# Moving one pair's casts and stores in tile one, and starting tile zero's small products with the other PSUM bank

## The chip, the cores and the metric

The kernel runs on one core of a Trainium2 chip. The metric is device time in microseconds: the median of the runs of one program, 899.4 us for the kernel before (899.08 to 900.18 in three runs).

## The reference, cut to what matters

Attention within chunks of 64 tokens, then RMS norm and a gated feed-forward layer. Everything is f32.

```python
# q, k, v: (8, 8, 576, 64); chunk = 64, 9 chunks per sequence
scores = scale * np.matmul(q_c, k_c.transpose(0, 1, 2, 4, 3))
scores = scores - np.max(scores, axis=-1, keepdims=True)
attn = np.exp(scores)
attn = attn / (np.sum(attn, axis=-1, keepdims=True) + 1e-09)
out = np.matmul(attn, v_c)
...
# x: (4608, 512), w_gate and w_val: (512, 1536), w_out: (1536, 512)
rms = np.sqrt(np.mean(x * x, axis=-1, keepdims=True) + 1e-06)
xn = x / rms * rms_g
g = xn @ w_gate
silu = g * (1.0 / (1.0 + np.exp(-g)))
val = xn @ w_val
return (silu * val @ w_out).astype(np.float32)
```

## The kernel before, in words

The 4608 tokens are nine tiles of 512. A tile holds the tokens of two *units* of 256; a unit u is loaded (`load_unit`, `load_values`), and its attention runs as scores, softmax, transposed weights, values, norm. Each matrix of the layer is split into a high and a low part (names ending in `h` and `l`), and every product is three matmuls of 128x512: high by high, high by low, low by high.

Tile zero is computed while the weights are still being converted (`conv_step`), and the order of its work is found by a scheduler that goes by priorities; in twelve *f* steps it makes `ps_g` and `ps_v` (L601), multiplies them and adds into four banks `acc` (L689). Units 2 and 3 are attended in it: their scores (L288), transposes (L349) and values (L472) are the *small products* between the large ones. Each of these slots writes two PSUM banks, one per half `j` of the partitions (`two_banks`: `banks[0]` for j = 0, `banks[1]` for j = 1), and `in_turn` holds the slot's instructions of units 2 and 3 in the order of the program. DVE reads the values out of the two banks in `norm_unit` (L521), two instructions for j = 0 and then two for j = 1.

Tiles one and two (`gated_pair`, L666) run in an order that is written out by hand, for PE, SP, DVE, ACT and POOL. They have 48 *steps* between them: a step is the twelve matmuls of one `ps_g` (even steps) or one `ps_v` (odd steps), and behind them whatever the tables put at that step. `ps_g` has two banks (pool `ps_h`), so the `ps_g` of step k+4 needs the `silu` (L679) of step k to be done; `ps_v` has four. The tables:

- `UNIT_AT`, one row for each of units 4 to 9: the steps of load, scores and softmax, load of the values, sums and first turn, two DMAs there and back through DRAM, values and norm (`turned_values`, `turned_norm`: L412, L426, L485), scaling, second turn, two more DMAs. The pool `ps_a` has two banks, which hold the scores of one unit or the values of another. So the next unit's scores wait until the norm of the unit before has let go of both: DVE scales the values out of them (L426), and ACT then squares into them (L485).
- `SUM_AT`, one row for each of six *pairs* i of output weights: sums on DVE (L719, L727), the split (ACT cast L731, DVE L732), the store `wol` (L736).
- `SIDE_AT`, one row for each of six pairs i of input weights: `whole` and `sums` on POOL (L755), then twice a split (ACT casts `side` L782, DVE `ab` L783) and its store `wsd` (L788, L789). `whole` takes a buffer from the pool `wts`, which hands out the buffers of earlier tiles as they come free.

`do` puts a closure at a step; those of one step run in the order in which they were entered (a step with .5 goes ahead of the following step's others). Units are entered first. All DMAs of these tables are issued by SP, in that order, and every engine runs its own queue in order. The lines that matter below, beside the functions that follow:

```python
        ri = mean_squares(halves, [st["o"].rearrange("p (a q) -> p a q", q=Q) for st in subs])
...
    ps_a = ctx.enter_context(tc.tile_pool(name="ps_a", bufs=2, space=bass.MemoryType.PSUM))
```

Of the kernel before, what the change touches and what calls it, by code (L numbers as in the profile page):

```python
# [48 lines left out]
)  # L49
SIDE_AT = (  # L50
    (1, 2, 3, 4, 3, 4),
    (6, 7, 7.5, 9, 9, 10),
    (10, 12, 14, 15, 16, 17),
    (15, 17, 19, 20, 21, 22),
    (25, 27, 29, 30, 31, 32),
    (30, 32, 34, 35, 36, 37),
# [20 lines left out]
NPR = NF // 2  # L77
# [32 lines left out]
def tile_chunk_attn_swiglu(  # L110
# [9 lines left out]
    nc = tc.nc  # L120
# [36 lines left out]
    def bank(pool, name):  # L157
        return pool.tile([P, 512], F32, tag=pool_tag[id(pool)], name=name)
# [3 lines left out]
    ident = const.tile([P, P], F32, name="ident")  # L162
# [81 lines left out]
    state = {}  # L244

    def load_unit(u):
        t = io.tile([P, 2, NPAIR, UT], F32, tag="qk", bufs=1, name="qk")
        nc.sync.dma_start(t, qk[u])
        for s in range(2):
            state[2 * u + s] = {"q": t[:, 0], "k": t[:, 1]}  # L250

    def load_values(u):
        vt = io.tile([P, NPAIR, UT // CH, D], F32, tag="io", name="vt")
        nc.sync.dma_start(vt, v[u])
        for s in range(2):
            state[2 * u + s]["v"] = vt
# [10 lines left out]
    def two_banks(pool, name):  # L267
        return [bank(pool, f"{name}{j}").rearrange("p (s c) -> p s c", s=2) for j in range(2)]
# [3 lines left out]
    def in_turn(i, ins):  # L272

        if 4 <= i < 8:
            if turn_last[0] is not None:
                info = mybir.DependencyInfo(mybir.DependencyClass.NoSync, mybir.DependencyReason.DATA)
                tc.add_manual_dep(ins.ins, turn_last[0].ins.name, info, reason="row groups take turns")
            turn_last[0] = ins

    def scores(i, banks):  # L280
        st, s = state[i], i % 2
        st["s"] = [b[:, s].rearrange("p (a k) -> p a k", k=CH) for b in banks]
        for pr in range(NPAIR):
            for j in range(2):
                for c in range(2):
                    tok = s * P + c * CH
                    rows = slice(j * D, (j + 1) * D)
                    ins = nc.tensor.matmul(  # L288
                        st["s"][j][c * CH : (c + 1) * CH, pr],
                        st["q"][rows, pr, tok : tok + CH],  # L290
                        st["k"][rows, pr, tok : tok + CH],
                        start=True,
                        stop=True,
                    )
                    in_turn(i, ins)
# [45 lines left out]
    def att_transpose(i, pool=None):  # L341
        st = state[i]
        e = st["e"].rearrange("p a j k -> p a (j k)")
        if i % 2 == 0:
            state["eT", i // 2] = att.tile([P, 2, NPAIR, P], F32, tag="eT", bufs=1, name="eT")
        eT = st["eT"] = state["eT", i // 2][:, i % 2]
        pt = bank(pool or ps_a, "ps_t").rearrange("p (a k) -> p a k", k=P)
        for pr in range(NPAIR):
            nc.tensor.transpose(pt[:, pr], e[:, pr], ident)  # L349
        nc.scalar.copy(eT, pt)  # L350


# [111 lines left out]
    def att_values(i, banks):  # L464
        st, s = state[i], i % 2
        eT, vt = st["eT"], st["v"]
        st["o"] = [b[:, s].rearrange("p (a d) -> p a d", d=D) for b in banks]
        for pr in range(NPAIR):
            for j in range(2):
                for c in range(2):  # L470
                    rows = slice(j * CH, (j + 1) * CH)
                    ins = nc.tensor.matmul(  # L472
                        st["o"][j][c * CH : (c + 1) * CH, pr, :],
                        eT[rows, pr, c * CH : (c + 1) * CH],
                        vt[rows, pr, 2 * s + c, :],
                        start=True,
                        stop=True,
                    )
                    in_turn(i, ins)
# [85 lines left out]
    def behind(ins):  # L565

        info = mybir.DependencyInfo(mybir.DependencyClass.Sync, mybir.DependencyReason.DATA)
        tc.add_manual_dep(ins.ins, split_last[0].ins.name, info, reason="tokens are split first")
        return ins
# [180 lines left out]
    def sides(i, st):  # L750

        at, ws = {}, []

        def total(out, one, two, op):
            return nc.gpsimd.tensor_tensor(out, one, two, op=op)  # L755

        def whole():
            ws = big([P, 2, 2, DM], F32, "ab")
            for f in range(2):
                hi, lo = (conv_parts[2 * i + f][:, n].bitcast(F32) for n in range(2))  # L760
                for half in range(2):
                    cols = slice(half * KH, (half + 1) * KH)
                    for m in range(2):
                        behind(total(ws[:, f, m, cols], hi[:, m, cols], lo[:, m, cols], ALU.add))
                    at[f + 1, half + 1] = ws[:, f, :, cols]

        def sums():
            for m in range(2):
                a = {n: w[:, m] for n, w in at.items()}
                total(a[2, 2], a[2, 1], a[2, 2], ALU.add)  # L770
                total(a[2, 1], a[1, 1], a[2, 1], ALU.subtract)
                total(a[1, 1], a[2, 2], a[1, 1], ALU.subtract)
                total(a[1, 2], a[1, 2], a[1, 1], ALU.subtract)

        forms = ((P7, (2, 1)), (P5, (2, 2))), ((P6, (1, 1)), (P3, (1, 2)))
        parts = {}

        def split(k):
            for p, n in forms[k]:
                w = at[n]  # L780
                part = parts[p] = st().tile([P, 2, KH], F32R, tag="side", bufs=4, name="side")
                nc.scalar.copy(part, w)  # L782
                nc.vector.tensor_tensor(w.bitcast(F32R), w, part.bitcast(F32), op=ALU.subtract)  # L783

        def save(k):
            for p, n in forms[k]:
                dst = wsd[:, 7 * i + p].rearrange("p (a m c) -> p a m c", a=2, m=2)
                nc.sync.dma_start(dst[:, 0], parts[p].bitcast(F32))  # L788
                nc.sync.dma_start(dst[:, 1], at[n])  # L789

        return [whole, sums, lambda: split(0), lambda: save(0), lambda: split(1), lambda: save(1)]

    def big(shape, dtype, name):
        return wts.tile(shape, dtype, tag="wts", name=name)
# [385 lines left out]
    for f in range(NF):  # L1180
        g = gated(f, CONVS[f % 2], conv_step)
        for u, at in enumerate(TILE1_AT, 2):
            if f == at[0]:
                load_unit(u)
                load_values(u)
                sc = two_banks(ps_a, "ps_s")
                for i in (2 * u, 2 * u + 1):
                    scores(i, sc)
                softmax_rows(u, sc)
            elif f == at[1]:  # L1190
                for i in (2 * u, 2 * u + 1):
                    att_transpose(i)
            elif f == at[2]:
                o = two_banks(ps_a, "ps_o")
                for i in (2 * u, 2 * u + 1):
                    att_values(i, o)
                scale[u] = norm_unit(u, o)
            elif f == at[3]:
                scale[u]()
        if f % 2:  # L1200
            save_out(f // 2)
        if f >= 6:
            save_up(f - 6)
        if f >= NF - 1 - EARLY_SUMS and f < NF - 1:
            for todo in out_sides(f - NF + 1 + EARLY_SUMS, lambda: wp.tile([P, 2 * DM], F32, name="w")):
                todo()
        if f == NF - 1:
            load_unit(4)
            x_transpose((0, 1))
        if prev is not None:  # L1210
            down(acc, f - 1, *prev)
        prev = g
# [19 lines left out]
    def do(k, f):  # L1232
        if k >= 4 * NF:
            down_at.setdefault(2 * (k - 4 * NF), []).append(f)
        elif k % 1:
            ahead.setdefault(int(k) + 1, []).append(f)
        else:
            at.setdefault(max(k, 0), []).append(f)
# [17 lines left out]
    for i in range(NPR):  # L1256
        for k, f in () if i < EARLY_SUMS else zip(SUM_AT[i], out_sides(i, lambda: st[0].tile([P, 2 * DM], F32, tag="ab", bufs=1, name="w"))):
            do(k, f)
        for k, f in zip(SIDE_AT[i], sides(i, lambda: st[0])):
            do(k, f)  # L1260
        do(P5_AT[i], lambda i=i: less_first(i))
# [31 lines left out]
    for b in range(-1, NB):  # L1293
# [7 lines left out]
        if not last_pair:  # L1301
            u = 2 * t + 4
# [98 lines left out]
```

## Time and profile before

| what | value |
|---|---|
| median of three runs | 899.4 us |
| the profiled execution's own time | 897.51 us |
| its span, first to last instruction | 895.7 us |
| PE busy | 874.6 us (98%) |
| DVE busy | 661.9 us (74%) |
| ACT busy | 438.7 us (49%) |
| POOL busy | 161.9 us (18%) |

The profiled execution lies 1.9 us below the median of the runs. A matmul's end is modelled, so PE's busy share says little; what is read in the prediction is the distance from one start to the next. In tiles one and two 128x512 matmuls start 0.23 us apart when nothing holds them up. In a row of the timeline the first number is the start in us from the beginning of the span, the second the length, and what stands in brackets is the time for which the engine sat idle ahead of it and what ended that. Rows of equal instructions are merged (x64).

### The profile page before, as it was taken

Reading aid. Unit: us, or ns where it says so; the run is one execution under the profiler, and the core shown is the slowest. Engines: PE = TensorE matmul, PEld = TensorE weight load, DVE = VectorE, ACT = ScalarE, POOL = GpSimd, SP = SyncE. Lnnn points to the kernel's source line nnn. Section 1 sums busy time; section 2 is a strip of 40 time slices with the busy share of each in tenths; the row PEclk is TensorE's granted clock in tenths of the full one; section 3 lists DMA queues with packets and bytes.
Section 4 is the critical chain, followed back from the end, with each engine's and each line's share of the span. In section 5 each row is a group of like instructions: output and inputs, shape, how many; then the busy total and the mean of one; then the engine's idle time right before and its main releaser. Section 6 shows DMA issues by size and latency. Waiting matters only on the chain.

```text
span 895.7 us, 17004 instructions
## 1 busy us (share of the span) xinstructions
PE 874.6 (98%) x6816; PEld 717.0 (80%) x6816; DVE 661.9 (74%) x971; ACT 438.7 (49%) x723; POOL 161.9 (18%) x185
## 2 busy tenths in 40 slices
PE   5899999999999999999999999999999999999998
PEld 4777878877888888888888888788888888888886
DVE  6899997877685887866757988666669973435885
ACT  5999955445452763333445644333546532112442
POOL 0000005666660000112220001222200012111000
PEclk9999999999999999999999999999999999999999
DMA  9698967789898867488986874898888687445523
GB/s 359 257 338 312 352 217 259 253 290 295 250 287 288 275 224 272 171 316 282 350 271 225 291 275 164 306 327 308 287 233 304 248 306 271 154 149 191 208 70 119
DMA packets 94495, 231.81 MB, mean 259 GB/s; under 512 B 7120, under 2 KB 63440, under 8 KB 79056
## 3 DMA queue, kind: packets, MB, share of 16 engines
q1 hardware_dynamic: 93360, 230.19, 73.8%
q8 instruction: 54, 0.88, 0.4%
q10 hardware_dynamic: 1056, 0.52, 0.2%
q14 instruction: 25, 0.20, 0.1%
HBM read 171.97 MB, written 58.72 MB: 258 GB/s over the span
## 4 chain that ended last, share of the span: by engine, by line
PE 78%; ACT 7%; DVE 6%; POOL 4%; DMA 3%; issue 2%; SPq 0%; ACTq 0%; DVEq 0%; POOLq 0%
PE ps_c L854 11%; PE ps_a L854 11%; PE ps_b L854 10%; PE ps_a L1035 7%; PE ps_b L1035 7%; PE ps_c L1035 7%; PE ps_d L854 6%; PE ps_g L666 4%; PE ps_v L666 4%; PE ps_d L1035 4%; POOL ab L755 3%; PE ps_o L412 2%; PE ps_s L288 2%; PE ps_g L601 1%; PE acc L689 1%
## 5 line engine op out<-in xcount | busy, mean ns | idle before, releaser
L954 ACT CAST gh<-g 128x512 fp32r<-128x512 f32 x140 | 81.7, 619 | 75.6 <-PE ps_b L1035 21.3
L955 DVE TENSOR_TENSOR gl<-g,gh 128x512 fp32r<-128x512 f32 x140 | 95.2, 686 | 30.8 <-ACT gh L954 29.7
L854 PE MATMUL ps_c<-xp,wr 128*128 128x512 f32 x432 | 104.6, 391 | 0.0
L854 PE MATMUL ps_b<-xp,wr 128*128 128x512 f32 x432 | 104.1, 390 | 0.0
L854 PE MATMUL ps_a<-xp,wr 128*128 128x512 f32 x432 | 103.5, 390 | 0.0
L854 PEld LDWEIGHTS ps_a<-xp,wr 128*128 128x128 f32 x432 | 80.9, 188 | 16.9
L854 PEld LDWEIGHTS ps_b<-xp,wr 128*128 128x128 f32 x432 | 80.8, 188 | 16.9
L854 PEld LDWEIGHTS ps_c<-xp,wr 128*128 128x128 f32 x432 | 80.6, 188 | 17.1
L919 POOL TENSOR_TENSOR g<-c,c 128x512 f32<-128x512 f32 x18 | 23.2, 1290 | 363.0 <-ACT c L895 175.2
L666 PE MATMUL ps_g<-xh,parts 128*128 128x512 f32 x192 | 65.1, 393 | 1.7 <-ACT sg L679 1.7
L666 PE MATMUL ps_v<-xh,parts 128*128 128x512 f32 x192 | 65.5, 394 | 0.0
L1035 PE MATMUL ps_a<-gh,wo 128*128 128x512 f32 x176 | 55.8, 389 | 0.0
L854 PE MATMUL ps_d<-xp,wr 128*128 128x512 f32 x216 | 52.3, 391 | 0.4 <-DMA wr<-wsd 0.4
L895 ACT ACTIVATE c<-c 128x512 f32<-128x512 f32 x18 | 11.4, 633 | 81.2 <-DVE c L915 81.1
L1035 PE MATMUL ps_c<-gh,wo 128*128 128x512 f32 x160 | 50.8, 391 | 0.0
L1035 PE MATMUL ps_b<-gh,wo 128*128 128x512 f32 x160 | 50.6, 389 | 0.0
L755 POOL TENSOR_TENSOR ab<-parts 128x256 f32<-128x256 f32 x48 | 41.9, 909 | 33.9 <-DVE xl L559 26.2
L854 PEld LDWEIGHTS ps_d<-xp,wr 128*128 128x128 f32 x216 | 40.3, 188 | 9.3 <-issue 0.8
L997 DVE TENSOR_TENSOR g<-g 128x512 f32<-128x512 f32 x68 | 46.4, 683 | 0.0
L904 DVE TENSOR_TENSOR u<-ps_b,p 128x512 f32<-128x512 f32 x36 | 24.6, 689 | 29.1 <-PE ps_b L854 24.1
L666 PEld LDWEIGHTS ps_g<-xh,parts 128*128 128x128 f32 x192 | 36.0, 188 | 9.9 <-ACT sg L679 2.1
L666 PEld LDWEIGHTS ps_v<-xh,parts 128*128 128x128 f32 x192 | 36.0, 188 | 7.9
(184 smaller groups left out, 1846.3 us busy)
## 6 DMA issues: line engine op xcount, KB each, us to landing
wr<-wsd SPq DMA_DIRECT2D x63, 1024.0 KB, 8.3
qk<-qk_dram SPq DMA_DIRECT2D x17, 1024.0 KB, 6.8
wo<-wol SPq DMA_DIRECT2D x16, 1024.0 KB, 9.0
raw<-w_up_dram SPq DMA_DIRECT2D x12, 1024.0 KB, 12.0
wo<-wod SPq DMA_DIRECT2D x12, 1024.0 KB, 8.9
vt<-v_dram SPq DMA_DIRECT2D x18, 512.0 KB, 7.8
wsd<-parts SPq DMA_DIRECT2D x18, 512.0 KB, 8.9
wo<-wol SPq DMA_DIRECT2D x16, 512.0 KB, 8.0
```

The lines of the kernel that those rows point to most:

```text
L288: ins = nc.tensor.matmul(st["s"][j][c * CH : (c + 1) * CH, pr], st["q"][rows, pr, tok : tok + CH], st["k"][rows, pr, tok : tok + CH], star ...
L412: nc.tensor.matmul(st["o"][(2 * c + t) * Q : (2 * c + t + 1) * Q, h * D : (h + 1) * D], eT[rows, c, t, h], vt[rows, c, h], start=True, sto ...
L666: nc.tensor.matmul(ps[k], a, b[dt], start=(dt == 0 and i == 0), stop=(dt == NDT - 1 and i == 2), skip_group_check=True,)
L755: return nc.gpsimd.tensor_tensor(out, one, two, op=op)
L854: nc.tensor.matmul(ps, w[:, a, m, cols], xp[:, b, kt], start=start and kt == 0 and i == 0, stop=stop and kt == 1 and i == 2, skip_group_ch ...
L895: nc.scalar.activation(t, t if src is None else src, AF.Silu)
L904: nc.vector.tensor_tensor(kp["u2"], b["b"], kp["p1"], op=add)
L919: nc.gpsimd.tensor_tensor(g[1][1], kp["c22"], kept[0]["c22"], op=mult)
L954: nc.scalar.copy(gh, src)
L955: nc.vector.tensor_tensor(gl, src, gh.bitcast(F32), op=ALU.subtract)
L997: nc.vector.tensor_tensor(out, one, two, op=ALU.subtract)
L1035: nc.tensor.matmul(ps[m][INTO[p]], w[:, m, a], parts[c], start=p in FROM and i == 0 and j == 0, stop=p in LAST and i == NPR - 1 and j == 2 ...
```

## The change

In `UNIT_AT` the fourth row (unit 7) loads its queries and keys at step 11 and not 12; its values and norm go from step 32 to 33, its scaling and second turn from 34 to 35, the store behind them from 35 to 36. In `SIDE_AT` the third row (pair 2) has its two splits at 16 and 17, not 14 and 16, and their stores at 17 and 18, not 15 and 17. All rows of `SUM_AT` are now entered ahead of all rows of `SIDE_AT`. In tile zero the small products of units 2 and 3 (i = 4 to 7) begin with j = 1, the transposes too are held in turn, and the second half of the unit is transposed first.

```diff
-    (12, 15, 27, 17, 19, 27, 32, 34, 34, 35, 38),
+    (11, 15, 27, 17, 19, 27, 33, 35, 35, 36, 38),
...
-    (10, 12, 14, 15, 16, 17),
+    (10, 12, 16, 17, 17, 18),
...
+    def halves_of(i):
+        return (1, 0) if 4 <= i < 8 else (0, 1)
...
         for pr in range(NPAIR):
-            for j in range(2):
+            for j in halves_of(i):
...
-        if i % 2 == 0:
+        if ("eT", i // 2) not in state:
...
-            nc.tensor.transpose(pt[:, pr], e[:, pr], ident)
+            in_turn(i, nc.tensor.transpose(pt[:, pr], e[:, pr], ident))
...
-                for i in (2 * u, 2 * u + 1):
+                for i in (2 * u + 1, 2 * u):
                     att_transpose(i)
...
     for i in range(NPR):
         for k, f in () if i < EARLY_SUMS else zip(SUM_AT[i], out_sides(i, ...)):
             do(k, f)
+    for i in range(NPR):
         for k, f in zip(SIDE_AT[i], sides(i, lambda: st[0])):
             do(k, f)
```

What this does to the queues is shown at three places. Lines of the changed kernel are three higher than those before. The first place is DVE in tile one, steps 7 to 9: `parts_775` is output pair 2, `ab_1762` input pair 1, `xu_1893` the norm of unit 4. Before, and then now:

```order
L727 TENSOR_TENSOR w_1796<-w_1796 128x256 x4
L783 TENSOR_TENSOR ab_1762<-ab_1762,side_1819 128x2x256
L783 TENSOR_TENSOR ab_1762<-ab_1762,side_1822 128x2x256
L732 TENSOR_TENSOR parts_775<-w_1796,parts_775 128x1024
L426 TENSOR_TENSOR xu_1893<-ps_o_1827,rs_u_1613 128x16x32
```

```order
L730 TENSOR_TENSOR w_1788<-w_1788 128x256 x4
L735 TENSOR_TENSOR parts_775<-w_1788,parts_775 128x1024
L786 TENSOR_TENSOR ab_1762<-ab_1762,side_1821 128x2x256
L786 TENSOR_TENSOR ab_1762<-ab_1762,side_1824 128x2x256
L429 TENSOR_TENSOR xu_1893<-ps_o_1827,rs_u_1613 128x16x32
```

The split of output pair 2 now stands ahead of the first split of input pair 1, and its store `wol` likewise on SP. The second place is ACT in steps 14 to 18: `e_128` is the softmax of unit 7, the `side` casts are those of input pair 2, `sg` is the `silu` of step 16. Before, and then now:

```order
L438 ACTIVATE xu_2101<-xu_2101,ri_t_2107 128x16x32 x2
L782 CAST side_2171<-ab_1995 128x512
L782 CAST side_2174<-ab_1995 128x512
L368 ACT_TABLE_LOAD
L368 ACTIVATE e_128<-e_128 128x1024
L679 ACT_TABLE_LOAD
L679 ACTIVATE sg_2250<-ps_g_2248 128x512
```

```order
L441 ACTIVATE xu_2103<-xu_2103,ri_t_2109 128x16x32 x2
L371 ACT_TABLE_LOAD
L371 ACTIVATE e_128<-e_128 128x1024
L682 ACT_TABLE_LOAD
L682 ACTIVATE sg_2240<-ps_g_2238 128x512
L785 CAST side_2261<-ab_1995 128x512
```

The four casts now stand behind that `silu`; on DVE `ab_1995` has likewise gone behind the softmax of unit 7. The third place is DVE in steps 31 to 34: `ab_2535` is input pair 4, `w` and `parts_1313` output pair 5, `xu` the norm of unit 7, `mx_u` the softmax of unit 9. Before, and then now:

```order
L783 TENSOR_TENSOR ab_2535<-ab_2535,side_2736 128x2x256
L426 TENSOR_TENSOR xu_2822<-ps_o_2756,rs_u_2294 128x16x32
L426 TENSOR_TENSOR xu_2822<-ps_o_2757,rs_u_2294 128x16x32
L719 TENSOR_TENSOR w_2837<-parts_1313 128x1024
L727 TENSOR_TENSOR w_2837<-w_2837 128x256 x4
L681 TENSOR_TENSOR g_2739<-ps_v_2741,sg_2742 128x512
```

```order
L786 TENSOR_TENSOR ab_2535<-ab_2535,side_2736 128x2x256
L722 TENSOR_TENSOR w_2758<-parts_1313 128x1024
L730 TENSOR_TENSOR w_2758<-w_2758 128x256 x4
L684 TENSOR_TENSOR g_2739<-ps_v_2741,sg_2742 128x512
L429 TENSOR_TENSOR xu_2855<-ps_o_2789,rs_u_2284 128x16x32
L429 TENSOR_TENSOR xu_2855<-ps_o_2790,rs_u_2284 128x16x32
```

The norm of unit 7 now stands behind the sums of output pair 5, where it stood ahead of them. On PE the values of unit 7 have gone from behind the `ps_g` of step 32 to behind the `ps_v` of step 33, and the scores of unit 9 still follow the `ps_g` of step 34. On SP the load of unit 7 has the same neighbours as before, since no DMA stood between its old place and its new one.

More of the change, by code (lines that the diff above doesn't have):

```diff
@@ L468, in att_values @@
         for pr in range(NPAIR):
-            for j in range(2):
+            for j in halves_of(i):
                 for c in range(2):
```

## The prediction

> **What bounds the kernel now.** I read the page first, then the waits of PE, then PE's timeline at the places that the change touches, and there the timelines of the engines that PE waits for.
>
> ```profile
> span 895.7 us, 17004 instructions
> PE 874.6 (98%) x6816; PEld 717.0 (80%) x6816; DVE 661.9 (74%) x971; ACT 438.7 (49%) x723; POOL 161.9 (18%) x185
> ```
>
> PE's waits, of all the span behind its first 40 us, the largest sum (us in total, times, longest):
>
> ```profile
> PE ps_g L666 <- ACT sg L679: 1.7, 1, 1.7
> ```
>
> PE is the bound, and with six smaller rows those waits add to 4.7 us. No matmul is added or removed. So the change is worth what it takes from these few waits, less the new ones that it makes. PE in tiles one and two, at the touched places:
>
> ```profile
> 178.40 1.39 PE L288 MATMUL ps_s<-qk 64*64 64x64 f32 x64
> 179.72 0.50 PE L666 MATMUL ps_v<-xh,parts 128*128 128x512 f32 x1
> ...
> 196.08 1.16 PE L288 MATMUL ps_s<-qk 64*64 64x64 f32 x64 [0.81 <-DMA qk<-qk_dram]
> ...
> 210.09 0.50 PE L666 MATMUL ps_g<-xh,parts 128*128 128x512 f32 x1 [1.72 <-ACT sg L679]
> 210.42 0.39 PE L666 MATMUL ps_g<-xl,parts 128*128 128x512 f32 x1
> ...
> 256.15 1.16 PE L288 MATMUL ps_s<-qk 64*64 64x64 f32 x64
> 257.24 0.50 PE L666 MATMUL ps_v<-xh,parts 128*128 128x512 f32 x1
> ```
>
> These are, in order, the scores of unit 6 (step 10), those of unit 7 (step 15, 0.81 us late for their load), the `ps_g` of step 20 (1.72 late) and the scores of unit 9 (step 34). Scores take 1.16 where nothing disturbs them; those of unit 6 took 1.39, so they were held in their middle for 0.23.
>
> **Term A, scores of unit 6.** That hold is for their second PSUM bank.
>
> ```profile
> 172.43 1.80 DVE L727 TENSOR_TENSOR w<-w 128x256 f32<-128x256 f32 x4
> 174.15 1.28 DVE L783 TENSOR_TENSOR ab<-ab,side 128x512 fp32r<-128x512 f32 x2
> 175.35 1.23 DVE L732 TENSOR_TENSOR parts<-w,parts 128x1024 fp32r<-128x1024 f32 x1
> 176.49 1.28 DVE L426 TENSOR_TENSOR xu<-ps_o,rs_u 128x512 f32<-128x512 f32 x2
> ```
>
> ```profile
> 174.26 1.05 ACT L731 CAST parts<-w 128x1024 fp32r<-128x1024 f32 x1 [1.21 <-DVE w L727]
> ```
>
> ```profile
> 177.87 0.60 ACT L485 ACTIVATE ps_o<-xu 128x512 f32<-128x512 f32 x1
> ```
>
> The norm of unit 4 starts at 176.49, its second square ends at 178.47, and the `ps_v` behind the scores starts at 179.72, 1.25 later. Now DVE does L732 first. That waits for the cast that ends at 175.31, so it starts at 175.35 as before; the two `ab`, which filled the gap, come behind it and push the norm by their distance, 175.35 - 174.15 = 1.20. Squares and bank move by as much: PE loses 1.2 us. Bounds: 0.9 if part of the `ab` still fits in the gap, 1.3 for their whole length.
>
> **Term B, the load of unit 7.** Moved from step 12 to 11 it passes no DMA on SP, so it starts no sooner.
>
> ```profile
> 180.43 2.04 SPq L736 DMA_DIRECT2D wol<-parts  x2
> ```
>
> ```profile
> 187.74 0.61 SPq L248 DMA_DIRECT2D qk<-qk_dram  x1
> ```
>
> SP spent 7.3 us on these two `wol` and five more issues between the rows; now `wol` goes ahead of all eight `wsd` stores, not between them, with the same bytes ahead of the load. So I leave the load where it was. PE comes 1.2 later by term A, more than the 0.81, and the wait is gone: a gain of 0.8. Bounds: 0 if the load lands as much later, 0.9 with the slower start behind a wait.
>
> **Term C, step 20.** The chain behind its 1.72 us:
>
> ```profile
> 187.40 7.02 POOL L755 TENSOR_TENSOR ab<-parts 128x256 f32<-128x256 f32 x8 [7.71 <-DMA wol<-parts]
> ```
>
> ```profile
> 197.99 1.25 DVE L444 STREAM_TRANSPOSE xu<-xu 128x1024 f32<-128x1024 f32 x1 [0.48 <-ACT xu L438]
> ```
>
> ```profile
> 201.29 1.14 ACT L782 CAST side<-ab 128x512 fp32r<-128x512 f32 x2 [3.33 <-POOL ab L755]
> ```
>
> ```profile
> 207.06 1.06 ACT L368 ACTIVATE e<-e 128x1024 f32<-128x1024 f32 x1 [3.33 <-DVE e L362]
> ```
>
> ```profile
> 209.44 0.60 ACT L679 ACTIVATE sg<-ps_g 128x512 f32<-128x512 f32 x1
> ```
>
> POOL waits until `wol` of pair 2 has landed, the casts wait for POOL, DVE's `ab` waits for the casts ahead of the softmax of unit 7, and the `silu` of step 16 waits for that softmax. Now casts and `ab` stand behind. DVE is through with its turn at 199.24; then come one L681 and the softmax's four instructions, some 0.6 to 0.7 each (3.4 in all), so the exponential starts near 202.7, not 207.06, and the `silu`, 2.38 behind it as before, near 205.1. PE asks for it at 210.09 - 1.72 = 208.4: it is 3 us early. The gain is 1.7, with the slower restart (0.33 instead of 0.23 to the next start, and some hundredths of semaphore time) 1.9. Bounds: 1.7 and 2.0. That `wol` and so POOL come sooner only widens this.
>
> **Term D, the turn to tile two.**
>
> ```profile
> 221.12 0.39 PE L666 MATMUL ps_g<-xh,parts 128*128 128x512 f32 x1
> 221.59 0.50 PE L666 MATMUL ps_g<-xl,parts 128*128 128x512 f32 x1
> ```
>
> The second matmul starts 0.47 behind the first, not 0.23: ACT's split of the new tile comes behind casts of pair 3, which had waited for POOL and for stores. With POOL sooner I take a gain of 0.2; pair 2's stores are a step later, so the bounds are 0 and 0.4.
>
> **Term E, scores of unit 9.** The values of unit 7 end one step ahead of the scores that need their two banks, not two, and the norm has gone behind the sums of pair 5.
>
> ```profile
> 252.77 1.28 DVE L426 TENSOR_TENSOR xu<-ps_o,rs_u 128x512 f32<-128x512 f32 x2
> 253.97 1.21 DVE L719 TENSOR_TENSOR w<-parts 128x1024 f32<-128x1024 f32 x1
> 255.21 2.22 DVE L727 TENSOR_TENSOR w<-w 128x256 f32<-128x256 f32 x4
> 257.35 0.68 DVE L681 TENSOR_TENSOR g<-ps_v,sg 128x512 f32<-128x512 f32 x1
> ```
>
> ```profile
> 192.10 3.06 DVE L727 TENSOR_TENSOR w<-w 128x256 f32<-128x256 f32 x4
> ```
>
> ```profile
> 256.18 7.49 POOL L755 TENSOR_TENSOR ab<-ab 128x256 f32<-128x256 f32 x8
> ```
>
> Until 252.77 nothing differs relative to PE. Then L719 and L727 take 253.97 to 257.35, which is 3.4, and L681 0.6, so the norm starts at 256.75. By term A's distances its squares end 1.98 later and the next `ps_v` starts 1.25 after that, at 259.98, where it was 257.24: PE loses 2.7. But POOL's sums no longer wait for this norm, so they run beside DVE's from the start; beside POOL (187.40 and on) four L727 took 3.06, against 1.80 with POOL idle and 2.22 here. With 3.06 the loss is 3.6. I take 3.4, nearer to that since POOL is busy throughout; bounds 2.7 and 4.0. Nothing gives it back: the list of waits has none of PE between here and 292 us to take it from.
>
> **Term F, tile zero.** The values of unit 2 were cut in two pieces and are now one.
>
> ```profile
> 76.42 0.33 PE L288 MATMUL ps_s<-qk 64*64 64x64 f32 x4
> ```
>
> ```profile
> 75.90 1.08 DVE L521 TENSOR_TENSOR x<-ps_o,rs_u 128x256 f32<-128x256 f32 x3
> ```
>
> ```profile
> 81.94 0.60 ACT L643 ACTIVATE sg<-ps_g 128x512 f32<-128x512 f32 x1 [0.18 <-PE ps_g L601]
> ```
>
> ```profile
> 96.21 1.23 DVE L229 TENSOR_TENSOR parts<-w,parts 128x1024 fp32r<-128x1024 f32 x1 [0.18 <-ACT parts L223]
> ```
>
> ```profile
> 126.06 0.74 PE L601 MATMUL ps_g<-xh,parts 128*128 128x512 f32 x2 [0.24 <-DVE parts L229]
> ```
>
> That saves a change of shape. But the scores of unit 3 are still cut after their first few, and the first piece now asks for the bank of j = 1. Of the three reads in the DVE row the first is the last of j = 0, the others are j = 1: with 1.08 for three, bank 0 is free at 76.3 and bank 1 at 76.98, 0.67 later. DVE sets that time, so PE stands until 0.67 later than before, and whatever the values won is lost in that wait. The delay goes on through ACT, which waits for PE at 81.94, to DVE, which waits for ACT at 96.21, to PE, which waits for DVE at 126.06. I take a loss of 0.6; bounds 0 (ACT or DVE has slack on the way) and 0.7. That the transposes of unit 3 are cut once more I cost at nothing: the two banks they write are their own. Tile one's DMAs start from PE and shift along.
>
> **Sum.** A +1.2, B -0.8, C -1.9, D -0.2, E +3.4, F +0.6: +2.3 us. Against the profiled execution's 897.5 that is 899.8; against the median of 899.4, from which this execution lies 1.9 below, 901.7.
>
> **Rivals.**
>
> 1. *No wait at the scores of unit 9.* If DVE reaches the norm of unit 7 by 254.0 (256.75 - 2.74), E is nothing: 898.3, not slower; between 254.0 and 256.75 it is in part. For it speaks that DVE's casts of pair 4 just ahead wait for POOL, which the change makes earlier in tile one; against it that POOL's work on that pair begins behind the norm of unit 6, which waits for PE, so that an earlier POOL does not move it:
>
> ```profile
> 230.72 0.34 POOL L487 TENSOR_SCALAR ms<-ms 128x2 f32<-128x2 f32 x1 [14.48 <-ACT ps_o L485]
> ```
>
> 2. *The load of unit 7 lands later.* With `wol` first, it costs from 0.4 of delay on (1.2 - 0.81); at 1.4 of delay B is +0.2 and not -0.8: 902.7. For it speaks SP's slow pace, against it the equal bytes.
>
> 3. *POOL shuts DVE out.* If each of DVE's five sums of pair 5 waits for a whole POOL operation of 7.49 / 8 = 0.94, the norm comes 1.21 + 1.80 + 4.7 + 0.6 behind 252.77, E is 7.1, and the time 905.4. Against it: the four at 192.10 lost 1.26, not 3.7. [...]
>
> 4. *PE slows behind its wait.* E would be the longest wait since the start. If the twelve matmuls behind it start twice as far apart, 12 x 0.23 = 2.7 is added: 904.4. Against it: behind 1.72 us the next start came after 0.33. [...]
>
> **How the numbers follow.** Forecast 0.63, rival 1 0.21 (in whole or part), rival 2 0.08, rival 3 0.03, rival 4 0.05. A change under 0.2% (1.8 us) can hardly be told from none. The forecast's bounds, A to F all low (0.9 - 0.9 - 2.0 - 0.4 + 2.7 + 0) and all high (1.3 + 0 - 1.7 + 0 + 4.0 + 0.7), are +0.3 and +4.3: 899.7 to 903.7. Rival 1 reaches down to 896.9 with F at 0. I take 898.4 to 903.4, which leaves out half of rival 1, the forecast's last corner, and rivals 3 and 4. Slower by over 0.2% (above 901.2): 0.6 of the forecast, and rivals 2 to 4, 0.54; less for rival 1's upper part taken as likelier, 0.50. Faster by as much (below 897.6): over half of rival 1's whole case, 0.12. No difference: 0.38.
>
> **What would show it.** The `ps_g` of step 20 without idle time; scores of unit 6 near 2.4 us long or later by 1.2, those of unit 7 without a wait for their load; scores of unit 9 held for 2.7 us or more, with the norm of unit 7 on DVE behind the sums of pair 5; `wol` of pair 2 ahead of its `wsd` neighbours and POOL's next sums 2 to 4 us sooner; in tile zero one piece of values of unit 2, and PE idle for some 0.9 ahead of the scores of unit 3. I am wrong above all if DVE reaches the norm of unit 7 early, or if PE's later start in tile one moves the loads less than PE.

## The result and the profile after

The changed kernel takes 905.33 us (median of 6 runs), the kernel before 899.24: a ratio of 1.0070, 95% interval 1.0052 to 1.0089, and outside the forecast range of 898.4 to 903.4. Measured again beside the experiments it took 903.36 against 898.57: 1.0044 (1.0030 to 1.0059). So the change costs 4 to 6 us. The side was forecast, the size (+2.3) was not. The second comparison lies at the upper edge of that range; why the two sets of six runs differ by 2 us stays open.

Two executions of the changed kernel were recorded, with spans of 905.3 and 901.5 us against 895.7 before. The page of the first, and PE's two largest waits in it behind the first 40 us (us in total, times, longest):

```profile
span 905.3 us, 17007 instructions
PE 878.2 (97%) x6816; PEld 720.4 (80%) x6816; DVE 665.2 (73%) x971; ACT 438.8 (48%) x723; POOL 160.7 (18%) x185
...
PE ps_s L291 <- ACT ps_o L488: 4.9, 3, 3.8
PE ps_s L291 <- DMA qk<-qk_dram: 2.2, 1, 2.2
```

The wait at the `ps_g` of step 20 is gone from this list. Of the two waits ahead of scores (L291 is L288 before) the first is new, and the second was 0.81 before. PE's timeline at the places that the prediction named, in the first recorded execution:

```profile
179.13 0.33 PE L291 MATMUL ps_s<-qk 64*64 64x64 f32 x4 [0.70 <-ACT ps_o L488]
179.79 1.15 PE L291 MATMUL ps_s<-qk 64*64 64x64 f32 x60 [0.33 <-ACT ps_o L488]
180.87 0.50 PE L669 MATMUL ps_v<-xh,parts 128*128 128x512 f32 x1
...
196.06 0.39 PE L669 MATMUL ps_v<-xh,parts 128*128 128x512 f32 x1
198.68 1.42 PE L291 MATMUL ps_s<-qk 64*64 64x64 f32 x64 [2.24 <-DMA qk<-qk_dram]
200.03 0.79 PE L669 MATMUL ps_g<-xh,parts 128*128 128x512 f32 x1
200.62 0.63 PE L669 MATMUL ps_g<-xl,parts 128*128 128x512 f32 x1
...
257.51 0.39 PE L669 MATMUL ps_g<-xh,parts 128*128 128x512 f32 x1
261.73 2.59 PE L291 MATMUL ps_s<-qk 64*64 64x64 f32 x64 [3.82 <-ACT ps_o L488]
264.24 0.79 PE L669 MATMUL ps_v<-xh,parts 128*128 128x512 f32 x1
264.83 0.63 PE L669 MATMUL ps_v<-xl,parts 128*128 128x512 f32 x1
```

Unit 6's scores come late by term A (`ps_v` at 180.87, not 179.72). Unit 7's wait for their load 2.24 us, and the large matmuls behind them start 0.59 and then 0.43 us apart, where 0.23 is usual. Unit 9's wait 3.82 us, take 2.59 instead of 1.16, and the matmuls behind them are slow in the same way. The windows of half a microsecond at the edges of these slow stretches (the third number from the end of a row is PE's granted clock):

```profile
199.00:199.50 0.50, 0.50 (x48) 0.50 (x42) 0.50 (x1) 0.50 (x2) 0.42 (x2) 0.91 0.15 57
202.50:203.00 0.50, 0.50 (x3) 0.39 (x2) 0.47 (x2) 0.00 (x0) 0.50 (x2) 0.68 0.93 352
260.50:261.00 0.50, 0.00 (x0) 0.00 (x0) 0.50 (x2) 0.05 (x1) 0.50 (x1) 0.85 1.06 219
267.50:268.00 0.50, 0.50 (x4) 0.41 (x2) 0.00 (x0) 0.50 (x1) 0.00 (x0) 0.82 0.03 6
```

Between these edges the granted clock is 0.50. A mean of 0.91 over half a microsecond with 1.0 ahead and 0.5 behind puts the fall at 199.41; by the same working it rises at 202.82, falls at 260.85 and rises at 267.68. In the recorded execution of before its mean from 40 to 895 us is 1.00. That is one execution: over whole executions, the first 40 us included, the mean clock of before lies between 0.994 and 1.000 in the 29 that ran beside the first experiments, and that of the changed kernel between 0.994 and 0.998 in all twelve.

DVE and POOL ahead of unit 9's scores:

```profile
254.49 1.75 DVE L722 TENSOR_TENSOR w<-parts 128x1024 f32<-128x1024 f32 x1
256.27 3.45 DVE L730 TENSOR_TENSOR w<-w 128x256 f32<-128x256 f32 x4
259.64 0.68 DVE L684 TENSOR_TENSOR g<-ps_v,sg 128x512 f32<-128x512 f32 x1
260.24 1.27 DVE L429 TENSOR_TENSOR xu<-ps_o,rs_u 128x512 f32<-128x512 f32 x2
```

```profile
255.12 5.99 POOL L758 TENSOR_TENSOR ab<-ab 128x256 f32<-128x256 f32 x6
```

The norm of unit 7 (L429) stands behind the sums as forecast, but these take 5.15 us up to the product behind them (254.49 to 259.64), not the 3.38 of before: the four L730 start 0.87 us apart on average, and so do POOL's instructions beside them (256.91 to 258.65).

**Where the time went.** The table compares the start of the same matmul (by its number on PE) with that before, in the recorded executions. Each column is what PE lost in that stretch: up to the end of tile zero, from there to behind unit 6's scores (A), behind unit 7's (B), the `ps_g` of step 20 (C), the turn to tile two (D), then all the rest but the stretch of unit 9's scores (E). The sum is the difference of the spans. Kernels that appear further down stand in it too.

| recorded execution | tile 0 | A | B | C | D | E | rest | sum |
|---|---|---|---|---|---|---|---|---|
| forecast | +0.6 | +1.2 | -0.8 | -1.9 | -0.2 | +3.4 | 0 | +2.3 |
| after, first | -0.0 | +1.2 | +3.0 | -1.9 | -0.4 | +7.0 | +0.7 | +9.6 |
| after, second | 0.0 | +1.2 | -0.1 | -1.9 | +0.2 | +6.6 | -0.2 | +5.8 |
| after_values32 | +0.2 | +1.2 | -0.9 | -1.9 | +0.9 | 0.0 | +0.5 | 0.0 |
| after_pool33 | +0.6 | +1.2 | -0.9 | -1.9 | +0.9 | +4.5 | +0.9 | +5.3 |
| after_sums33 | 0.0 | +1.2 | -0.9 | -1.9 | +0.8 | +0.2 | -0.1 | -0.8 |
| after_fill | +0.8 | +1.2 | +1.2 | -1.9 | -0.4 | +4.6 | -0.4 | +5.0 |
| after_values32_fill | 0.0 | +1.2 | +0.3 | -1.9 | -0.3 | +3.6 | -0.7 | +2.3 |
| before_loops | +0.3 | +1.2 | -0.4 | -1.3 | +0.7 | 0.0 | +0.2 | +0.8 |
| before_zero | +0.4 | 0.0 | +0.8 | -1.1 | -0.3 | 0.0 | +2.2 | +2.0 |
| before_side | +0.6 | 0.0 | +1.1 | -1.9 | -0.4 | 0.0 | +2.3 | +1.6 |
| before_side_load | -0.1 | 0.0 | -0.9 | -1.9 | +1.0 | 0.0 | -0.3 | -2.1 |
| before_side_load2 | 0.0 | 0.0 | -0.9 | -1.9 | -0.4 | 0.0 | +1.7 | -1.6 |

Of the tile zero column, up to 0.8 is scatter ahead of 40 us; the rest column is mostly waits of later tiles for a load of weights (`wr`) or ahead of a unit's values, which come and go from one execution to the next. The recorded execution of before (897.51 us) lies 1.7 below the median of the six runs of before, so the sums come out higher than the measured differences. E alone exceeds the measured slowdown.

### The profile page after: what moved, and what is told of

Its sections match the earlier page's. It is cut to its first block, busy times and chain, and to the rows that moved or that the text cites. A ratio compares the mean times of both kernels' runs of the same rounds, so it can differ in the third digit from the quotient of the medians.

```text
span 905.3 us, 17007 instructions
## 1 busy us (share of the span) xinstructions
PE 878.2 (97%) x6816; PEld 720.4 (80%) x6816; DVE 665.2 (73%) x971; ACT 438.8 (48%) x723; POOL 160.7 (18%) x185
## 4 chain that ended last, share of the span: by engine, by line
PE 66%; DMA 2%; ACT 1%; DVE 1%; SPq 0%; issue 0%; POOL 0%; ACTq 0%
PE ps_c L857 10%; PE ps_b L857 10%; PE ps_a L857 10%; PE ps_b L1038 7%; PE ps_a L1038 7%; PE ps_c L1038 7%; PE ps_d L857 5%; PE ps_d L1038 4%; PE ps_v L669 2%; PE ps_g L669 2%; PE ps_o L415 1%; DMA wr<-wsd 1%; PE ps_s L291 1%; DMA away_x<-xu 1%; DMA x<-away_x 0%
## 5 line engine op out<-in xcount | busy, mean ns | idle before, releaser
L758 POOL TENSOR_TENSOR ab<-parts 128x256 f32<-128x256 f32 x48 | 40.0, 871 | 31.0 <-DVE xl L562 26.2
```

## The experiments

**The changed kernel once more.**

> The changed kernel once more, for a second profiled execution. Theory 1 (the load of unit 7 lands too late by an amount that varies, and the clock falls behind each long wait of PE): the time is again about 905.3 us with a spread of 3 us or more, the scores of unit 9 wait 3.8 us again because DVE and POOL set that wait, but the wait for the load of unit 7 differs from 2.24 us by up to 1.5 us, and where it is under about 1.7 us (the wait that left the granted clock at 1.0 before the change) the clock stays at 1.0 behind it. Theory 2 (the order of the stores fixes the landing): the load is late by 2.2 us again, within 0.2.

903.36 us, ratio 1.0044 (1.0030 to 1.0059). Unit 9's scores waited 3.76 us, within 0.1 of the first time, and the clock fell again (0.50 from 257.74 to 264.56). The wait for the load of unit 7 was 0.69 and not 2.24, and the clock stayed at 1.0 there: the execution's mean of 0.996 is what the 6.82 us at 0.50 make of it by themselves. PE at unit 9:

```profile
255.19 0.39 PE L669 MATMUL ps_g<-xh,parts 128*128 128x512 f32 x1
259.33 2.58 PE L291 MATMUL ps_s<-qk 64*64 64x64 f32 x64 [3.76 <-ACT ps_o L488]
```

In the trace this is theory 1. The times are not what it expected: they are 2 us lower, and spread over 1.4 us, not 3. From issue to landing this load took, by the trace, 10.1 and 9.3 us in these two executions, 8.2 before, and 7.7 to 10.4 in the other kernels where it has the same neighbours on SP.

**Term E undone, in two ways.** The values of unit 7 back at their step:

```diff
-    (11, 15, 27, 17, 19, 27, 33, 35, 35, 36, 38),
+    (11, 15, 27, 17, 19, 27, 32, 34, 34, 35, 38),
```

> The changed kernel with the values and the norm of unit 7 (and its scaling, second turn and store) put back to their steps before, 32, 34, 34 and 35. Theory 1 (the move of this norm costs 2.7 for DVE's sums ahead of it, 1.8 for their slowing beside POOL, 2.4 for the fallen clock, 6.9 us in all): no wait at the scores of unit 9, the granted clock stays at 1.0 there, and the time is 905.3 - 6.9 = 898.4 us. Theory 2 (the forecast's 3.4 for this term was right and the rest went elsewhere): 901.9 us.

897.07 us, ratio 0.9979 (0.9968 to 0.9991): 6.3 us less than the changed kernel, and a little faster than before. No wait at unit 9's scores, clock 1.0:

```profile
255.67 1.16 PE L291 MATMUL ps_s<-qk 64*64 64x64 f32 x64
256.76 0.50 PE L669 MATMUL ps_v<-xh,parts 128*128 128x512 f32 x1
```

Then the values at step 33 as changed, but DVE's sums of output pair 5 behind them:

```diff
-SUM_AT = (), (), (7, 7.5, 9), (12, 13, 15), (26, 27, 29), (32, 33, 35)
+SUM_AT = (), (), (7, 7.5, 9), (12, 13, 15), (26, 27, 29), (33, 34, 35)
```

> The changed kernel with DVE's sums of output pair 5 at step 33 and its split at 34, so that the norm of unit 7 goes ahead of the five sums, with the values still at step 33. Theory 1 (the order of norm and sums on DVE is the whole of the lost 6.9 us): no wait over 0.5 us at the scores of unit 9, the granted clock at 1.0, and about 6.7 us less than the changed kernel, 896.7 us. Theory 2 (the values that end one step later cost by themselves, or the sums then hold the softmax of unit 9 and PE waits behind it): a wait of 1 us or more there or within five steps, 898 to 901 us.

897.57 us, ratio 0.9993 (0.9980 to 1.0005). DVE in it:

```profile
252.50 1.27 DVE L429 TENSOR_TENSOR xu<-ps_o,rs_u 128x512 f32<-128x512 f32 x2
253.70 1.46 DVE L722 TENSOR_TENSOR w<-parts 128x1024 f32<-128x1024 f32 x1
255.19 3.46 DVE L730 TENSOR_TENSOR w<-w 128x256 f32<-128x256 f32 x4
```

The sums are nearly as slow beside POOL as in the changed kernel (4.9 us up to the instruction behind them, 253.70 to 258.58, where it was 5.15), but behind the norm they cost PE 0.2 us at most. So neither the later values nor the slow sums cost by themselves: it is the norm's place behind the sums.

**POOL's part of E.**

```diff
-    (30, 32, 34, 35, 36, 37),
+    (30, 33, 34, 35, 36, 37),
```

> The changed kernel with one number moved: POOL's sums of input pair 5 at step 33 and not 32, so that they stand behind the norm of unit 7 as before the change, and DVE's sums of output pair 5 run with POOL idle in part. Theory 1 (POOL slows those five DVE instructions): L722 and the four L730 take 3.4 us again and not 5.15, the wait at the scores of unit 9 falls from 3.8 to about 2.0 us, and the time is 1.8 us less by the wait alone (903.5), up to 4.2 us less if the granted clock stays at 1.0 too (901.1). Theory 2 (they are slow from DMA or from their own place): their lengths and the time stay, 905.3 us.

901.66 us, ratio 1.0034 (1.0014 to 1.0055), 1.7 below the changed kernel; the intervals overlap, so the trace has to carry the verdict. DVE and then PE in it:

```profile
252.58 1.74 DVE L722 TENSOR_TENSOR w<-parts 128x1024 f32<-128x1024 f32 x1
254.36 1.80 DVE L730 TENSOR_TENSOR w<-w 128x256 f32<-128x256 f32 x4
256.08 0.68 DVE L684 TENSOR_TENSOR g<-ps_v,sg 128x512 f32<-128x512 f32 x1
```

```profile
258.17 0.33 PE L291 MATMUL ps_s<-qk 64*64 64x64 f32 x4 [2.12 <-ACT ps_o L488]
258.79 1.71 PE L291 MATMUL ps_s<-qk 64*64 64x64 f32 x60 [0.28 <-ACT ps_o L488]
260.43 0.79 PE L669 MATMUL ps_v<-xh,parts 128*128 128x512 f32 x1
```

With POOL idle the four L730 take 1.80 again and the sums 3.50 in all; the wait is 1.7 shorter, as theory 1 has it. But behind a wait of 2.12 us the clock still fell (0.50 from 259.14 to 262.56): the last 60 scores take 1.71 and not 1.15, and the matmul behind them starts the slow stretch.

**The clock's part of E.** Sixteen matmuls that nobody reads, in the place where PE stands idle:

```diff
+            if dt == NDT - 1 and k == "g" and half.n == 34:
+                for m in range(16):
+                    nc.tensor.matmul(ps["v"], wvh[f][:, 0:P], xh[0], start=m == 0, stop=m == 15, ...)
```

> The changed kernel with sixteen more 128x512 matmuls on PE just ahead of the scores of unit 9, into the bank that the ps_v of step 35 then overwrites; nobody reads them. 16 x 0.227 = 3.6 us of work in a wait of 3.8 us. Theory 1 (PE's clock falls because PE stood idle, and that costs 0.8 us in the scores and 1.2 to 1.6 us in the matmuls behind them): the wait shrinks to 0.2 us, the granted clock stays at 1.0, the scores behind it take 1.7 us and not 2.5, and the kernel is 2.0 us FASTER than the changed kernel although it does more, 901.4 us. Theory 2 (the slow matmuls behind the wait have another cause, or the filling delays the norm): 903.4 us or more.

> The same sixteen matmuls in the kernel whose values of unit 7 are back at step 32, where PE has no wait there to hide them in. Both theories: 897.1 + 3.6 = 900.7 us. Below 900 us another wait behind it would have taken some of them.

PE in after_fill, where L681 is the new matmul:

```profile
256.74 3.79 PE L681 MATMUL ps_v<-xh,parts 128*128 128x512 f32 x16
260.72 0.33 PE L291 MATMUL ps_s<-qk 64*64 64x64 f32 x4 [0.20 <-ACT ps_o L488]
261.33 1.15 PE L291 MATMUL ps_s<-qk 64*64 64x64 f32 x60 [0.28 <-ACT ps_o L488]
262.41 0.50 PE L669 MATMUL ps_v<-xh,parts 128*128 128x512 f32 x1
262.75 0.39 PE L669 MATMUL ps_v<-xl,parts 128*128 128x512 f32 x1
```

after_fill took 901.61 us, ratio 1.0022 (1.0002 to 1.0041), where the changed kernel's was 1.0044 (1.0030 to 1.0059): the intervals overlap, but the rows are plain. With PE kept at work the clock stays at 1.0 (1.00 from 254 to 266 us), the scores and the matmuls behind them run at their usual pace, and E is 4.6 in the table, not 6.6 to 7.0; from the first score to the next `ps_v` it is 1.69 us, not 2.51. Over all its executions the mean clock was 1.000 in nine of twelve and 0.998 in three. Where there is no wait to hide them, the same matmuls took the kernel from 897.07 to 900.72 us (ratio 1.0024, 1.0006 to 1.0042), as expected. So 2.0 to 2.4 us of E are the fallen clock; the 4.6 left are, within 0.1, the 2.7 of the order on DVE and the 1.8 of POOL.

**The other terms by themselves**, each put into the kernel before.

> The kernel before with all rows of SUM_AT entered ahead of all rows of SIDE_AT, and nothing else. Theory 1 (terms A and B as forecast): the scores of unit 6 are held 1.2 us longer behind the norm of unit 4, the 0.8 us wait for the load of unit 7 goes into that, and the time is 0.4 us above before. Theory 2 (the load lands later by what the load before it and its own latency vary, so that B gives nothing): 1.2 us above before, with a wait for that load of 0.5 to 2 us.

898.93 us, ratio 1.0008 (0.9993 to 1.0023): A is +1.2 in the trace, B (-0.4) and C (-1.3) give back more than that, and D takes 0.7; not to be told from no change, nor theory 1 from theory 2 by the time.

> The kernel before with the part of the change in tile zero alone. Theory 1 (term F as forecast, a loss handed on through ACT and DVE): 0.6 us above before. Theory 2 (the wait ahead of the scores of unit 3 is paid out of the slot of values that is no longer cut in two, and evens out by the turn): within 0.2 us of before; the turn to tile one comes 0.0 to 0.1 us earlier.

898.81 us, ratio 1.0002 (0.9988 to 1.0017), and in the trace PE, 0.5 us late at 40 us by scatter, reaches the turn 0.4 late. So tile zero lost nothing from there on: theory 2. In the changed kernel's tile zero:

```profile
76.41 0.33 PE L291 MATMUL ps_s<-qk 64*64 64x64 f32 x4 [0.53 <-issue]
```

```profile
75.90 1.08 DVE L524 TENSOR_TENSOR x<-ps_o,rs_u 128x256 f32<-128x256 f32 x3
```

The first piece of unit 3's scores starts at 76.41 as before, while DVE reads the values of j = 1 until 76.98. So the scores of j = 1, which the program puts first, do not write where those values lie: they got the bank that DVE left first. PE stands 0.53 us ahead of them, 0.4 more than before, but by the uncut values it had come 0.4 sooner.

> The kernel before with the third row of SIDE_AT alone changed (splits of input pair 2 at 16 and 17, stores at 17 and 18). Theory 1 (the forecast's term C is right by itself): the 1.72 us wait at the ps_g of step 20 is gone and the time falls by 1.9 us, 897.4 us. Theory 2 (the later stores take it back at the turn to tile two or at the load of unit 7): 899.2 us, with a new wait there.

```diff
-    (10, 12, 14, 15, 16, 17),
+    (10, 12, 16, 17, 17, 18),
```

897.79 us, ratio 0.9988 (0.9976 to 1.0001). In the trace C is -1.9 to the tenth, yet the time falls by 0.8. That is between the two theories. In the recorded execution (899.15 us, above the median of its runs) the load of unit 7 came 1.1 us later relative to PE than in that of before, and PE kept that loss. In before_zero, with the wait of step 20 still there, the load came 0.8 later and step 20 gave all of it back (-1.1). So, as far as these two executions show, the 1.72 us were not all PE's to win: they also took up whatever the load was late.

**A version that beats both.** With the row above, the load of unit 7 ahead of the eight stores of input pair 1:

```diff
-    (12, 15, 27, 17, 19, 27, 32, 34, 34, 35, 38),
+    (11, 15, 27, 17, 19, 27, 32, 34, 34, 35, 38),
...
-    (6, 7, 7.5, 9, 9, 10),
+    (6, 7, 7.5, 11, 9, 11),
```

> The kernel before with the third row of SIDE_AT changed, and on SP the load of unit 7 (step 11) ahead of the eight stores of input pair 1, which go to step 11 too. Theory 1 (the load is late because SP and the DMA engines serve those stores first): the load is issued 3 us or more sooner, no wait of PE for it, 0.8 us off on top of term C's 1.9, and so 2.5 to 3 us below before, 896.0 us. Theory 2 (the later stores hold POOL's buffer or a later load instead): as the kernel with the row of SIDE_AT alone, 897.8 us, with a wait in another place.

895.27 us, ratio 0.9967 (0.9953 to 0.9981), the fastest. SP issues the load 4.8 us sooner than before, it lands after 6.8 us, and PE does not wait:

```profile
182.96 0.42 SPq L248 DMA_DIRECT2D qk<-qk_dram  x1
```

Now 1.0 us goes at the turn to tile two. ACT there:

```profile
216.33 0.62 ACT L782 CAST side<-ab 128x512 fp32r<-128x512 f32 x1 [0.19 <-DMA wsd<-side]
217.63 0.62 ACT L782 CAST side<-ab 128x512 fp32r<-128x512 f32 x1 [0.68 <-DMA wsd<-side]
218.16 1.34 ACT L555 ACTIVATE xh<-x,g_col 128x512 fp32r<-128x512 f32 x2
```

The casts of input pair 3 wait until the stores of pair 2, now later, have landed, and hold the split of the new tile (L555) that PE needs. So the last try moved these casts:

```diff
-    (15, 17, 19, 20, 21, 22),
+    (15, 17, 20, 21, 24, 25),
```

> The fastest kernel so far (the row of SIDE_AT for pair 2, and the load of unit 7 ahead of the stores of pair 1) with the two splits of input pair 3 at steps 20 and 24 and not 19 and 21, their stores at 21 and 25. Theory 1 (PE's 1.0 us at the turn to tile two comes from ACT's casts of pair 3, which wait for the later stores of pair 2 to free the four side buffers, and hold the split of the new tile): the waits for xh and xl at 218 to 219 us fall from 1.0 to 0.3 us or less, 894.6 us. Theory 2 (the split of the new tile is held by its own data): the waits stay, 895.3 us.

The waits at the turn are gone (D -0.4 and not +1.0), but the time is 895.97 us, ratio 0.9956 (0.9940 to 0.9972), not to be told from the version ahead of it: 2.0 us of waits for later weights came up in its recorded execution.

## Why the prediction was right or wrong

- **Term A** was right: +1.2 in all recorded executions with it.
- **Term C** was right in the trace (-1.9) and wrong as a gain: "the gain is 1.7" took a wait off the sum that in other executions had been covering the late load.
- **Term B** failed at "so I leave the load where it was". That took one landing, 8.2 us after its issue, for a constant. It is 7.7 to 10.4, and B came out between -0.9 and +3.0. The case of rival 2 (a load that lands later) is thus not a way in which the change goes, but something that happens in some executions; in the first recorded one it also brought the clock down, 1.3 us in the matmuls alone.
- **Term D** failed at "with POOL sooner I take a gain": it came out between -0.4 and +1.0. In both recorded executions of the changed kernel ACT's casts of pair 3 wait for the stores of pair 2 and end at 219 to 220 us, hardly sooner than before (220.1). PE, 2.1 late, lost nothing by that in the first; in after_values32, where it came 1.5 early, it lost 0.9. The later stores had been named, and priced only as a smaller gain. They are not the whole of it: in before_loops they stand at their steps of before, the casts wait for them too, and D is +0.7.
- **Term E** was mis-sized, and is the step on which the forecast broke: 3.4 forecast (2.7 to 4.0), 6.6 to 7.0 measured. The order on DVE was right and gives 2.7. For POOL beside DVE the forecast took 0.7, it was 1.8; the pace of the four L727 beside POOL before (3.06) was taken for all of it, where L722 grew by 0.5 too and the L730 to 3.45. The rest, 2.0 to 2.4, is the clock. Rival 4 had this cause, near its true size (2.7), and 5 chances in 100. That starts come twice as far apart was a supposition, which no row of before shows; the runs showed 0.43 us between starts instead of 0.23, at a granted clock of 0.50, for 3.41 to 6.83 us. What was held against it, that behind 1.72 us nothing slowed, says nothing on a wait twice as long, and the wait that the forecast itself put there was one.
- **Rival 3** (POOL shuts DVE out wholly, E of 7.1) came to the same number in another way: DVE's five sums took 5.15 us, not the 7.7 that it gives them. That the time it named, 905.4, was met is luck. That a sum waits for a whole POOL operation (0.94) the trace does not show: the L730 start 0.87 us apart beside POOL, one to each of its instructions, and 0.46 without (L727 at 172.43 before). Each started with some 0.55 us of a POOL instruction still to run and took 0.84 instead of 0.42, so it lost 0.4.
- **Rival 1** (no wait at unit 9's scores) did not occur.
- **Term F** failed at "the first piece now asks for the bank of j = 1". The names in the order do not say which bank a tile gets; by the rows above the first-used tile got the bank that came free first, and tile zero lost nothing.

In the second recorded execution, A to D came to -0.7 (forecast -1.7), tile zero to 0.0 (+0.6) and E to 6.6 (3.4): the miss is E, with the clock the largest part that was left out.

## What to carry to other kernels

When a wait is about to become the longest that the matmul engine has, price the clock behind it as part of the likeliest case (2.0 to 2.4 us here); a trace with short waits alone cannot speak against it. A wait that vanishes is worth only what no other late arrival was hiding in it, so look for the loads and stores just ahead of it, and for the next engine that will be late, before taking it as a gain. And when two tables put sums and a norm at the same step, what goes first on the queue decides more than the step does.

## What the runs showed of the hardware

Each stretch of tiles one and two in which the granted clock was 0.50, with its edges by the working above, and PE's wait ahead of it:

| recorded execution | PE idle from | for | clock falls | rises | at 0.50 for |
|---|---|---|---|---|---|
| after, first | 196.44 | 2.24 | 199.41 | 202.82 | 3.41 |
| after, first | 257.91 | 3.82 | 260.85 | 267.68 | 6.83 |
| after, second | 255.57 | 3.76 | 257.74 | 264.56 | 6.82 |
| after_pool33 | 256.05 | 2.12 | 259.14 | 262.56 | 3.42 |

The edges in the second execution, and then those in after_pool33, are from these rows:

```profile
257.50:258.00 0.50, 0.00 (x0) 0.00 (x0) 0.50 (x2) 0.00 (x0) 0.42 (x2) 0.74 1.15 172
264.50:265.00 0.50, 0.50 (x3) 0.38 (x2) 0.23 (x1) 0.20 (x1) 0.00 (x0) 0.94 1.01 342
```

```profile
259.00:259.50 0.50, 0.50 (x36) 0.50 (x32) 0.00 (x0) 0.50 (x1) 0.42 (x2) 0.64 0.70 113
262.50:263.00 0.50, 0.50 (x3) 0.42 (x3) 0.47 (x2) 0.00 (x0) 0.50 (x1) 0.94 1.02 346
```

The four stretches thus have two lengths, 3.41 to 3.42 us and 6.82 to 6.83. The clock fell 2.17 to 3.09 us behind the start of the wait: at 260.85 and 257.74 while PE still stood idle, at 199.41 and 259.14 when it was at work on the scores again. In these tiles waits of 1.9 us (before_side, at unit 7) and 2.0 us (after_fill, at unit 7) went by with the clock at 1.00, and each wait from 2.12 us on was followed by a fall. Whether the length of a wait settles it by itself, and where between 2.0 and 2.12 us a border would then lie, no run shows.

In the first recorded execution the clock fell, and stayed down, while small matmuls ran. Unit 7's 64 scores of 64x64 had been running since 198.68 when it fell at 199.41. Unit 9's ran from 261.73 to 264.24 at 0.50, and the clock rose at 267.68, 3.44 us into the large matmuls behind them. In the second execution large matmuls ran until 255.57, 2.17 us ahead of the fall at 257.74.
